# Block-sparse attention with an MLP behind it: the newest value block of each sparse slot issued by SyncE in place of GpSimd

## The chip, the cores and the metric

One core of a Trainium2 chip runs the whole program. The metric is the device time of one execution in microseconds (us); smaller is better. Engines are named as the profile names them: PE (TensorE; PEld is its weight load), DVE (VectorE), ACT (ScalarE), POOL (GpSimd), SP (SyncE). SP computes nothing here: it issues DMAs, one after the other, and waits ahead of each for what the DMA needs.

## What is computed

Attention over 4 batches, 8 heads, 768 tokens and a head width of 64, with a mask in blocks of 32 tokens, and behind it an MLP on the 3072 token rows.

```python
mask = np.abs(blk_i - blk_j) <= 1                     # a window of three blocks
mask = mask | (blk_i == 0) | (blk_j == 0) | (blk_i == n_blocks - 1) | (blk_j == n_blocks - 1)
for qb in range(n_blocks):
    for kb in sampled_blocks[qb]:                     # three sampled blocks for each query block
        mask[qb * 32:(qb + 1) * 32, kb * 32:(kb + 1) * 32] = True
attn = softmax(where(mask, q @ k.T / 8, -1e9))
x = (attn @ v) as rows of 512
out = (s * relu(x @ w_in) ** 2 + b) @ w_out           # 512 -> 2048 -> 512
```

## The kernel before

The work has two stages. The attention stage fills the first 235 us or so, the MLP the rest.

**Slots.** Attention runs in 52 slots, numbered from 0 in the order of the string `T["ORD"]`. Eight are dense (the first and the last query block of a batch, which see every key). The other 44 are sparse: one query block `k` of two batches (a pair `e` of batches) at a time. The sparse query blocks of a pair run in three streams A, B and C (`r` is 0, 1 or 2), taken in turns, and each stream steps by one block. So the window of three neighbours of a stream's next block differs from the last one's by one block: the newest neighbour. The first slot of a stream (`entire`) loads all three neighbours, each later one only the newest. A slot is 4 units (two batches, two parities of heads).

**What a sparse slot does.** PE makes the scores (L979), DVE takes the maximum and adds the mask (L997), ACT the exponential (L1010), PE transposes the probabilities (L1040), DVE and ACT in turn copy them out of PSUM (L1056, L1058), and PE multiplies them with the values (L1106). DVE scales the result (L1112), PE transposes it (L1121), ACT copies it (L1126, tile `xst`), and SP spills it to DRAM (L1133). In one slot of eight blocks there are products with the dense slots' probabilities as well (L1096).

**Values.** Tile `vA` holds one row of three neighbour blocks for each stream and one row of sampled blocks; `vB` holds four more rows of sampled blocks. The window row of a stream is used again by its next slot, three sparse slots later, with one third of it replaced. So the newest neighbour of slot i can be loaded only when the value products of the stream's last slot have read the row. Five rows for sampled blocks go round. `window_v` (L791) issues the load of one neighbour block, 128 KB: for an `entire` slot SP does (21 loads), for the others POOL (38 loads). `sampled_v` (L884) issues the three sampled blocks of a slot: two by SP and the third by POOL, from slot 7 on (L1266).

**What else the two engines issue.** POOL also copies the keys of each slot into `kk` (L913, L924), loads the queries of the sparse slots (L731) and takes part in the decoding of the weights (L88). SP also loads the second pair's keys in 12 pieces during slots 5 to 16 (L714), the queries of the dense slots (L731), the weights (L59, L62), and the attention's results back for the MLP (L401).

**Order.** Each engine works through a fixed list. The lists come from a planner in the kernel, `Plan` (L109): each operation is entered with an engine, a cost in ns, a due time, what it depends on, and what buffers it takes; `Plan.order` then plays the program through with these costs and writes down the order in which things would start. An engine that comes free takes, of what could start first, the one that is due first. The line for the window loads is L1262: on SP and POOL alike the cost is 650, the due time 11 units ahead of the slot (`T["VL"]`). The sampled loads (L1267) are due 13 units ahead and cost 850 on SP. Nothing in the plan runs on the chip: there each engine takes its list in order, and waits at each entry until semaphores say that it may go.

Of the kernel before, what the change touches and what calls it, by code (L numbers as in the profile page):

```python
# [108 lines left out]
class Plan:  # L109
# [15 lines left out]
    def op(self, eng, cost, prio, fn, deps=(), alloc=(), use=(), order=(), nbytes=0, cols=0, late=0.0):  # L125


        o = Plan.Op()
        o.cost, o.prio, o.fn, o.nbytes, o.cols, o.late = cost if isinstance(cost, dict) else {eng: cost}, prio, fn, nbytes, cols, late
        o.pick = isinstance(cost, dict)  # L130
        o.deps, o.order, o.alloc = [d for d in deps if d], [d for d in order if d], alloc
        o.end, o.seq = None, len(self.ops)
        for k in (*alloc, *use):
            self.users.setdefault(k, []).append(o)
        self.ops.append(o)
        return o
# [76 lines left out]
def kernel(  # L213
# [16 lines left out]
    nc = tc.nc  # L230
# [449 lines left out]
    with ExitStack() as es:  # L680
# [12 lines left out]
        for w in T["ORD"].split():  # L693
            if w[1] == "D":
                slots.append(("d", "abcd".index(w[0]), int(w[2]), 0))
            else:
                r = "ABC".index(w[1])
# [37 lines left out]
        def value_tiles():  # L735
            if "A" not in vbox:
                for z in "AB":
                    vbox[z] = gp.tile([P, 4, 2, DM], F32, tag="vg", name=f"v{z}", bufs=2)

        def window_values(r):  # L740
            value_tiles()
            return vbox["A"][:, r]
# [16 lines left out]
        def block_rows(e, j, n=1):  # L759

            return v[2 * e:2 * e + 2, j * BLK:(j + n) * BLK, :].rearrange("a r d -> r a d")

        def newest(k):
            return k - 1 if STREAMS[1] >= k > STREAMS[1] - 8 else k + 1
# [23 lines left out]
        def newcomers(k, entire):  # L788
            return list(range(k - 1, k + 2)) if entire else [newest(k)]

        def window_v(i, entire, m):  # L791

            _, e, k, r = slots[i]
            js = newcomers(k, entire)
            j, p = (js[m], js[m] % 3) if m < len(js) else (0, NSL)
            (nc.sync if entire else nc.gpsimd).dma_start(out=window_values(r)[p::4], in_=block_rows(e, j))


        ident = pers.tile([P, P], F32, name="ident")
# [106 lines left out]
        def window_k(i, entire):  # L906

            _, e, k, r = slots[i]
            kk = keys_tile()
            if entire:  # L910
                nc.gpsimd.tensor_copy(flat(kk[:, r, NSL:NSL + 1]), flat(kts[e][:, :1]))
            for j, p, n in runs(k, entire):
                nc.gpsimd.tensor_copy(flat(kk[:, r, p:p + n]), flat(kts[e][:, j:j + n]))  # L913

        def sampled_k(i, a):

            _, e, k, r = slots[i]
            row = ring_row("k", i)
            kg = keys_tile()[:, NST + row]
            if a == 0 and holds["k"].get(row) != e:  # L920
                holds["k"][row] = e
                nc.gpsimd.tensor_copy(flat(kg[:, NSL:]), flat(kts[e][:, NB - 1:]))
            j = block_register(mybir.EngineType.Pool, k, a)
            nc.gpsimd.tensor_copy(flat(kg[:, a:a + 1]), flat(kts[e][:, bass.ds(j, 1)]))  # L924
# [219 lines left out]
        op = plan.op  # L1144
# [47 lines left out]
        def parts_of(e, blocks):  # L1192
            return [kld[(e, y, p)] for p in sorted({j * KPS[e] // NB for j in blocks}) for y in range(2)]
# [11 lines left out]
        for i, (kind, e, k, r) in enumerate(slots):  # L1205
            u, cost, col = unit_of[i], costs[kind], cols[kind]
# [3 lines left out]
            def queries(which=(0, 1), after=None):  # L1210
                nonlocal pq
                if which[0] in lqs.setdefault(qk, {}):
                    return
                if not dense:
                    firsts.add(qk)
                for a in which:
                    for par in range(2):
                        fresh = not (a or par)
                        pq = op("s" if dense else "g", 450 if dense else 700, max(u - T["QL"], -18.0 if dense else -9.5 if len(firsts) < 3 else -4.5) + 0.01 * par + (9.5 * (u == 0) if dense else 0.02) * a,
                                lambda qk=qk, a=a, par=par: load_q(qk, a, par), alloc=[("qr", qk)] if fresh else [], use=[] if fresh else [("qr", qk)],  # L1220
                                order=[pq] if dense else [pq, after, o_rg if len(firsts) < 3 else first_pk], nbytes=131e3)
                        lqs[qk].setdefault(a, []).append(pq)
# [4 lines left out]
            if dense:  # L1227
                s_use.append((f"kt{e // 2}", e // 2))
            else:
                prev = before.get(r)  # L1230
                if qk[2] == 1:
                    queries((0,), lastk[sorted(lastk)[-2]])
                    queries((1,), pk)
                elif qk[2] == 2:
                    queries((0,), pk)
                entire = k == STREAMS[r]
                first = not before
                blocks = [*range(k - 1, k + 2), 0] if entire else [newest(k)]
                new = [("kk", "kk")] if first else []
                pk = op("g", 1900 if entire else 430, u - T["GK"], lambda i=i, w=entire: window_k(i, w),  # L1240
                        [*parts_of(e, blocks), *(prev[0] if prev else [])], alloc=new, use=[(f"kt{e}", e)] + ([] if first else [("kk", "kk")]), order=[pk])
                s_deps.append(pk)
                first_pk = first_pk or pk
                if qk[2] != 2:
                    queries()
                for a in range(NSL):
                    pk = op("g", 460, u - T["GK"] + 0.1 * (a + 1), lambda i=i, a=a: sampled_k(i, a), [o_rg, *parts_of(e, range(NB))],
                            alloc=[] if a else [("kg", i)], use=[(f"kt{e}", e), ("kk", "kk")] + ([("kg", i)] if a else []), order=[pk])
                    s_deps.append(pk)
                queries((1,), pk)  # L1250
                lastk[i] = pk
                s_use += [("kk", "kk"), ("kg", i)]

                vt = [("vg", "vA"), ("vg", "vB")]
                if first:
                    for m in range(5):
                        pvl = op("s", 450, -8.3 + 0.02 * m, lambda m=m: global_values(m), alloc=[] if m else vt, use=vt if m else [],
                                 order=[pvl], nbytes=(131e3 if m == 4 else 200e3))
                        globs.append(pvl)
                av_deps += globs if e == 0 else []  # L1260
                for m in range(len(newcomers(k, entire)) + (entire and e > 0)):
                    pvl = op("s" if entire else "g", 650, -8.2 + 0.02 * m if first else u - T["VL"] + 0.1 * m, lambda i=i, w=entire, m=m: window_v(i, w, m), prev[1] if prev else [],  # L1262
                             use=vt, order=[pvl], nbytes=131e3)
                    av_deps.append(pvl)
                for a in range(NSL):
                    bg = a == NSL - 1 and i > T["BG"]  # L1266
                    o = op("g" if bg else "s", 700 if bg else 850, u - T["GV"] + 0.1 * a, lambda i=i, a=a, bg=bg: sampled_v(i, a, bg), [o_rg if bg else o_rs],  # L1267
                           alloc=[] if a else [("vs", i)], use=[*vt, *([("vs", i)] if a else [])], order=[pvs], nbytes=131e3)
                    if not bg:
                        pvs = o  # L1270
                    av_deps.append(o)
                pv_at.append((u, pvs))
                if i in T["K1"]:
                    key_piece(1, None, T["K1"].index(i), u - T["GV"] + 0.4, [pvs, spills.get(([None] * 5 + sparse)[sparse.index(i)])])
                av_use = [*vt, ("vs", i)]
# [78 lines left out]
            if k % NBC == 1:  # L1354
                left = sum(sl[0] == "s" and sl[1] == e and sl[2] % NBC == 1 for sl in slots[i + 1:])
                done[e] = done.get(e, 0) + 1
                for b in (2 * e, 2 * e + 1):
                    g = (k - 1) // NBC // (NCK // 2)
# [96 lines left out]
        for k in range(NPL):  # L1455
            g, f = subs[k]
# [6 lines left out]
            if k > 0:  # L1463
                g, f = subs[k - 1]
# [46 lines left out]
    for i in range(NPL, NSUB):  # L1511
        g, f = subs[i]
# [12 lines left out]
    for s in range(S0, B):  # L1525
        a, b = 2 * s, 2 * s + 1
        for p in range(NFC // 2):
            for n in (1, 2, 6, 7, 5, 3, 4):
                to = product(p, s, n)
                i = None  # L1530
# [4 lines left out]
                elif n == 2:  # L1535
                    i = take((a, p), to, part_sums["m1"], ALU.add)
# [4 lines left out]
                elif n == 5:  # L1541
                    i = take((b, p + 8), to, part_sums["u2"], ALU.add)
                    vec.tensor_tensor(out=part_sums["u3"], in0=to, in1=part_sums["u1"], op=ALU.add)  # L1543
                elif n == 3:
                    i = take((b, p), to, part_sums["u3"], ALU.add)
                else:
                    i = take((a, p + 8), part_sums["u2"], to, ALU.subtract)
# [93 lines left out]
```

## Time and profile before

| | us |
|---|---|
| time, median of 3 runs | 752.07 (748.76 to 755.04) |
| time of the profiled execution | 755.85 |
| its span, first to last instruction | 754.2 |
| PE busy | 732.4 (97%) |
| DVE busy | 568.8 (75%) |
| ACT busy | 471.3 (62%) |
| POOL busy | 286.7 (38%) |

Some 1.65 us of the profiled execution's time lie around its span. Waiting and the issue of DMAs aren't counted as busy, so POOL's share says nothing of how long it was held up by either, and SP has no share at all. Matmuls overlap, and PE counts as busy while any of them runs, so PE can be busy and still run below its best pace.

### The profile page before, as it was taken

How to read it: one execution, taken by the hardware profiler on the slowest of the kernel's cores; microseconds unless marked ns; L12 is line 12 of the kernel's file. 1: busy time of each engine (PE TensorE's matmuls, PEld its weight loads, DVE VectorE, ACT ScalarE, POOL GpSimd, SP SyncE). 2: the span in 40 equal slices, each digit the busy share in tenths (PEclk: the TensorE clock that was granted, in tenths of full speed). 3: DMA queues.
4: the chain of work that ended last, by engine and by line, in shares of the span. 5: the costliest groups of instructions: out<-in, count | busy, mean ns of one | idle time of the engine just before them, and what ended most of it. 6: DMA issues, size and time to landing. Idle time of an engine off the chain costs nothing.

```text
span 754.2 us, 21532 instructions
## 1 busy us (share of the span) xinstructions
PE 732.4 (97%) x8032; PEld 624.8 (83%) x8032; DVE 568.8 (75%) x1439; ACT 471.3 (62%) x1140; POOL 286.7 (38%) x477
## 2 busy tenths in 40 slices
PE   7898999999999999999999999999999999999997
PEld 6676766777778898998889888988989988898896
DVE  4866658988787899988886787787677688666752
ACT  3866557989686878788644433675434566345443
POOL 6966657767851221210023222232222322222221
PEclk9999999999999999999999999999999999999999
DMA  9998767867776345536322330233000022000002
GB/s 249 253 272 251 203 184 218 227 190 211 220 207 176 113 135 178 191 112 161 117 59 84 107 96 29 67 114 79 1 1 1 1 63 85 1 1 0 1 1 83
DMA packets 98888, 89.42 MB, mean 119 GB/s; under 512 B 50368, under 2 KB 79936, under 8 KB 98784
## 3 DMA queue, kind: packets, MB, share of 16 engines
q1 hardware_dynamic: 92544, 71.27, 32.5%
q0 software_dynamic: 6096, 16.65, 7.9%
q8 instruction: 63, 1.03, 0.6%
q14 instruction: 41, 0.34, 0.1%
q10 hardware_dynamic: 144, 0.13, 0.0%
HBM read 69.15 MB, written 14.68 MB: 111 GB/s over the span
## 4 chain that ended last, share of the span: by engine, by line
PE 88%; DVE 5%; ACT 3%; issue 2%; DMA 1%; SPq 1%; DVEq 0%; ACTq 0%
PE m L636 21%; PE o L490 11%; PE o L491 11%; PE o L489 11%; PE xs L1106 6%; PE t L1040 6%; PE s L979 6%; PE h L443 3%; PE h L445 3%; PE h L444 3%; PE od L1096 2%; PE t L1121 2%; PE t L1038 1%; DVE ptile L997 1%; PE s L958 1%
## 5 line engine op out<-in xcount | busy, mean ns | idle before, releaser
L467 POOL TENSOR_TENSOR hid<-hid,hid 128x384 fp32r<-128x384 f32 x96 | 105.2, 1096 | 295.8 <-ACT hid L654 286.2
L653 ACT ACTIVATE hid<-hid,sb_b,sb_s 128x384 f32<-128x384 f32 x96 | 68.0, 709 | 153.6 <-DVE hid L647 153.5
L1010 ACT ACTIVATE ptile<-ptile,nm 128x256 f32<-128x256 f32 (+1 forms) x208 | 107.5, 520 | 40.9 <-DVE nm L997 40.9
L997 DVE CUSTOM_DVE_ANT_1 ptile<-s,mt 128x256 f32<-128x256 f32 x176 | 64.4, 420 | 17.3 <-PE s L979 17.0
L491 PE MATMUL o<-woutr,hid 128*128 128x512 f32 x168 | 66.5, 396 | 0.0
L490 PE MATMUL o<-woutr,hid 128*128 128x512 f32 x168 | 66.3, 395 | 0.0
L489 PE MATMUL o<-woutr,hid 128*128 128x512 f32 x168 | 65.3, 389 | 0.0
L636 PE MATMUL m<-wout,win 128*128 128x384 f32 x264 | 61.9, 338 | 0.0
L636 PE MATMUL m<-xp,wop 128*128 128x384 f32 x288 | 58.3, 337 | 0.0
L647 DVE SCALAR_TENSOR_TENSOR hid<-hid 128x384 f32<-128x384 f32 x96 | 54.6, 569 | 3.3
L490 PE MATMUL o<-win,hid 128*128 128x512 f32 x144 | 56.8, 394 | 0.0
L636 PE MATMUL m<-xp,win 128*128 128x384 f32 x288 | 54.6, 337 | 1.4 <-DVE sum L1543 1.4
L1040 PE MATMUL t<-ident,ptile 128*128 128x128 f32 x352 | 54.5, 297 | 0.2
L636 PEld LDWEIGHTS m<-xp,win 128*128 128x128 f32 x288 | 50.9, 188 | 4.1 <-issue 1.7
L654 ACT CAST hid<-hid 128x384 fp32r<-128x384 f32 x96 | 49.4, 514 | 7.8 <-ACT hid L653 0.7
L636 PEld LDWEIGHTS m<-xp,wop 128*128 128x128 f32 x288 | 51.5, 188 | 2.1
L1040 PEld LDWEIGHTS t<-ident,ptile 128*128 128x128 f32 x352 | 45.8, 208 | 6.4 <-issue 0.7
L924 POOL COPY kk<-kt 128x256 f32 x132 | 50.6, 420 | 0.0
L1106 PE MATMUL xs<-vA,pt 128*32 128x64 f32 x1696 | 46.6, 224 | 3.7 <-issue 3.3
L491 PE MATMUL o<-win,hid 128*128 128x512 f32 x126 | 49.8, 395 | 0.0
L489 PE MATMUL o<-win,hid 128*128 128x512 f32 x126 | 49.2, 391 | 0.5 <-ACT ob L505 0.4
L646 DVE TENSOR_TENSOR hid<-m,xrest 128x384 f32<-128x384 f32 x48 | 26.5, 551 | 30.5 <-issue 26.4
(199 smaller groups left out, 1889.4 us busy)
## 6 DMA issues: line engine op xcount, KB each, us to landing
vB<-in_v_dram SPq DMA_DIRECT2D x76, 128.0 KB, 4.1
raw_o<-in_w_out_dram SPq DMA_DIRECT2D x14, 512.0 KB, 3.3
raw_i<-in_w_in_dram SPq DMA_DIRECT2D x12, 512.0 KB, 4.0
vA<-in_v_dram POOLq DMA_DIRECT2D x46, 128.0 KB, 3.6
xd<-xst SPq DMA_DIRECT2D x44, 128.0 KB, 3.7
vA<-in_v_dram SPq DMA_DIRECT2D x42, 128.0 KB, 4.6
sum<-xd SPq DMA_DIRECT2D x12, 384.0 KB, 3.9
out_dram<-ob SPq DMA_DIRECT2D x18, 256.0 KB, 2.3
```

Source lines behind the costliest of these rows:

```text
L467: (eng or nc.vector).tensor_tensor(out=htile(5 + i % 3), in0=t, in1=gh.bitcast(F32), op=ALU.subtract)
L489: nc.tensor.matmul(acc, gh[:, tsl], wout(f, 0), start=first, stop=False)
L490: nc.tensor.matmul(acc, gh[:, tsl], wout(f, 1), start=False, stop=False)
L491: nc.tensor.matmul(acc, gl[:, tsl], wout(f, 0), start=False, stop=last)
L636: nc.tensor.matmul(to, w_, x_, start=(c == 0 and k == 0), stop=(c == 1 and k == 2))
L647: vec.scalar_tensor_tensor(out=t, in0=t, scalar=0.0, in1=t, op0=ALU.max, op1=ALU.mult)
L653: nc.scalar.activation(t, t, AF.Identity, bias=sb_b, scale=sb_s)
L924: nc.gpsimd.tensor_copy(flat(kg[:, a:a + 1]), flat(kts[e][:, bass.ds(j, 1)]))
L997: nc.vector.tensor_tensor_reduce(out=pt, in0=sp, in1=msk, scale=-scale, scalar=FMAX if g == 0 else nm[:, 0:1], op0=ALU.add, op1=ALU.min, a ...
L1010: nc.scalar.activation(pt, pt, AF.Exp, bias=nms[n][:, last:last + 1], scale=-1.0, accum_out=dns[i][:, g, j:j + 1])
L1040: nc.tensor.transpose(tp[:, (2 * j + c) * P:(2 * j + c + 1) * P], src[:, c:SW:2], ident)
L1106: nc.tensor.matmul(xs[quads[pair]], pt[:, c, quads[pair]], vt[:, a, col:col + D], start=(j == 0 and c == 0), stop=(c == 1), tile_position= ...
```

## The change

The newest neighbour's value block of each sparse slot is issued by SP; the planner is told so with the same cost (650) and due time.

```diff
@@ window_v, L796 @@
-            (nc.sync if entire else nc.gpsimd).dma_start(out=window_values(r)[p::4], in_=block_rows(e, j))
+            nc.sync.dma_start(out=window_values(r)[p::4], in_=block_rows(e, j))
@@ the plan, L1262 @@
-                    pvl = op("s" if entire else "g", 650, -8.2 + 0.02 * m if first else u - T["VL"] + 0.1 * m, lambda i=i, w=entire, m=m: window_v(i, w, m), prev[1] if prev else [],
+                    pvl = op("s", 650, -8.2 + 0.02 * m if first else u - T["VL"] + 0.1 * m, lambda i=i, w=entire, m=m: window_v(i, w, m), prev[1] if prev else [],
```

All 38 window loads leave POOL's list and enter SP's. PE's list stays as it is; on DVE and ACT some operations of the weights' decoding and of the attention's end change places.

The first place is SP's list from the spill of slot 6 to that of slot 7. `xst6` is the block of slot 6 that is spilled, L714 a piece of the second pair's keys, and the two groups of L896 are two sampled blocks of slot 12, with the register work ahead of each. Before:

```order
L1133 DMA xd_68<-xst6_965 128x256
L714 DMA kt1_448<-in_k_blk_dram 128x2x256
L896 REGISTER_ALU x2
L896 ISA
L896 DMA vB_212<-in_v_dram 32x2x512
L896 REGISTER_ALU x2
L896 ISA
L896 DMA vB_212<-in_v_dram 32x2x512
L1133 DMA xd_68<-xst7_1061 128x256
```

And now:

```order
L1133 DMA xd_68<-xst6_963 128x256
L796 DMA vA_211<-in_v_dram 32x2x512
L714 DMA kt1_448<-in_k_blk_dram 128x2x256
L896 REGISTER_ALU x2
L896 ISA
L896 DMA vB_212<-in_v_dram 32x2x512
L896 REGISTER_ALU x2
L896 ISA
L896 DMA vB_212<-in_v_dram 32x2x512
L1133 DMA xd_68<-xst7_1060 128x256
```

The window load of slot 10 (L796) stands behind the spill of slot 6, and ahead of the key piece and the sampled blocks. Of the 38, 24 stand right behind the spill of an earlier slot.

The second place is SP's list near the end of attention, from the spill of slot 45 to that of slot 48. `xraw1_0` is a part of the attention's result on its way back for the MLP. Before:

```order
L1133 DMA xd_68<-xst45_4841 128x256
L896 REGISTER_ALU
L896 ISA
L896 DMA vB_212<-in_v_dram 32x2x512
L896 REGISTER_ALU x2
L896 ISA
L896 DMA vB_212<-in_v_dram 32x2x512
L1133 DMA xd_68<-xst46_4946 128x256
L1133 DMA xd_68<-xst47_5040 128x256
L401 DMA xraw1_0_5125<-xd_68 128x12x64
L1133 DMA xd_68<-xst48_5142 128x256
```

And now:

```order
L1133 DMA xd_68<-xst45_4839 128x256
L796 DMA vA_211<-in_v_dram 32x2x512
L896 REGISTER_ALU
L896 ISA
L896 DMA vB_212<-in_v_dram 32x2x512
L896 REGISTER_ALU x2
L896 ISA
L896 DMA vB_212<-in_v_dram 32x2x512
L1133 DMA xd_68<-xst46_4931 128x256
L796 DMA vA_211<-in_v_dram 32x2x512
L1133 DMA xd_68<-xst47_5047 128x256
L796 DMA vA_211<-in_v_dram 32x2x512
```

The first L796 is the window load of slot 48, the next two those of slots 49 and 50; each waits its turn behind a spill.

The third place is DVE's list where the first weights are decoded, between the dense slots in the middle of attention. `xss22` is slot 22's result, `raw_i0` the first piece of weights, `nm89` to `nm91` are the maxima of units 89 to 91, and `pt84` is the probabilities of slot 23. Before:

```order
L1112 TENSOR_TENSOR xss22_2512<-xs_613,rc22_2351 128x256
L85 TENSOR_SCALAR wkhp0_387<-raw_i0_2245 128x512
L87 TENSOR_SCALAR wklp0_534<-raw_i0_2245 128x512
L997 ISA ptile6_80,nm89_2480<-s89_1_2452,mz_114,nm89_2480 128x128x3
L997 ISA nm89_2480 128x1
L1056 COPY pt84_0_2553<-t84_0_2527 128x512
```

And now:

```order
L1112 TENSOR_TENSOR xss22_2513<-xs_613,rc22_2349 128x256
L85 TENSOR_SCALAR wkhp0_387<-raw_i0_2245 128x512
L997 ISA ptile6_80,nm89_2481<-s89_1_2452,mz_114,nm89_2481 128x128x3
L997 ISA nm89_2481 128x1
L1056 COPY pt84_0_2552<-t84_0_2527 128x512
L997 ISA ptile2_79,nm90_2564<-s90_2542,mt_116 128x256
L997 ISA nm90_2564 128x1
L997 ISA ptile2_79,nm91_2571<-s91_2543,mt_116 128x256
L997 ISA nm91_2571 128x1
L87 TENSOR_SCALAR wklp0_534<-raw_i0_2245 128x512
```

The second step of the decoding (L87) has moved behind the copy of slot 23's probabilities (L1056) and two more maxima.

## Rows read from the trace of the kernel before

**Rows 1.** The chain that ended last by engine; then two of the stretches (--windows).

```profile
PE 88%; DVE 5%; ACT 3%; issue 2%; DMA 1%; SPq 1%; DVEq 0%; ACTq 0%
...
core 0: us, PE busy (x) PEld busy (x) DVE busy (x) ACT busy (x) POOL busy (x), PEclk, DMA share, GB/s
...
60.00:80.00 20.00, 16.93 (x477) 12.12 (x467) 12.15 (x54) 12.88 (x46) 13.28 (x30) 1.00 0.87 246
...
160.00:180.00 20.00, 20.00 (x578) 15.22 (x585) 17.89 (x68) 15.86 (x53) 14.01 (x32) 1.00 0.69 207
```

**Rows 2.** Waits of PE, 20 to 240 us, the seven longest: us in total, times, longest.

```profile
PE xs L1106 <- issue: 5.1, 4, 1.8
PE t L1121 <- DVE pt L1056: 1.8, 4, 0.9
PE s L979 <- DVE rc L1019: 1.2, 1, 1.2
PE t L1038 <- DVE nm L997: 1.1, 2, 0.5
PE od L1096 <- issue: 0.9, 2, 0.5
PE od L1121 <- ACT xst L1126: 0.7, 1, 0.7
PE s L979 <- issue: 0.4, 1, 0.4
```

**Rows 3.** Waits of PE's weight loads, 20 to 240 us, for POOL and for loads.

```profile
PEld s L979 <- POOL kk L924: 1.3, 1, 1.3
...
PEld xs L1106 <- DMA vA<-in_v_dram: 0.3, 2, 0.2
```

**Rows 4.** Groups, 20 to 236 us: busy us, mean ns, idle before it.

```profile
L796 POOL DMA_DIRECT2D vA<-in_v_dram x38 | 21.0, 552 | 28.2 <-PE od L1096 20.3 <-PE xs L1106 7.5
```

**Rows 5.** Line L796: ns min/median/max; its DMAs to landing, both queues.

```profile
L796 SPq DMA_DIRECT2D vA<-in_v_dram x21: 598/605/1113, 16.2 to 144.5; - x21
...
DMA to landing us min/median/max: 2.4/4.0/10.7
```

**Rows 6.** DMA issues of value blocks: KB each, median us to landing.

```profile
vB<-in_v_dram SPq DMA_DIRECT2D x76, 128.0 KB, 4.1
...
vA<-in_v_dram POOLq DMA_DIRECT2D x46, 128.0 KB, 3.6
...
vA<-in_v_dram SPq DMA_DIRECT2D x42, 128.0 KB, 4.6
```

**Rows 7.** Timeline of SP from slot 6's spill to slot 7's: start, us.

```profile
51.39 1.16 SPq L1133 DMA_DIRECT2D xd<-xst  x1
52.60 0.43 SPq L714 DMA_DIRECT2D kt<-in_k_blk_dram  x1
53.43 1.55 SPq L896 DMA_DIRECT2D vB<-in_v_dram  x2
55.09 0.53 SPq L1133 DMA_DIRECT2D xd<-xst  x1
```

**Rows 8.** Timelines of POOL (slot 10's window load) and PE (slot 10's first value product).

```profile
49.59 0.55 POOL L796 DMA_DIRECT2D vA<-in_v_dram  x1 [0.41 <-PE xs L1106]
...
59.53 0.32 PE L1106 MATMUL xs<-vA,pt 128*32 128x64 f32 x8
```

**Rows 9.** Timelines of SP (slot 45's spill) and PE (slot 48's value products).

```profile
215.64 1.32 SPq L1133 DMA_DIRECT2D xd<-xst  x1
...
221.69 1.29 PE L1106 MATMUL xs<-vA,pt 128*32 128x64 f32 x64
```

**Rows 10.** Timelines of DVE and PE where the first weights are decoded.

```profile
119.05 1.39 DVE L87 TENSOR_SCALAR wklp<-raw_i 128x512 uint16<-128x512 uint16 x1
...
121.60 0.44 PE L1121 MATMUL t<-ident,xss 128*128 128x128 f32 x2 [0.94 <-DVE pt L1056]
```

**Rows 11.** Waits of SP, 30 to 235 us: us in total, times, longest.

```profile
SPq L1133 <- ACT xst L1126: 34.8, 22, 3.7
```

## The prediction

> **What bounds the kernel now.** I read the chain of waits first, because it says which engine the end hangs on: PE holds 88% of it, and no other engine more than 5% [rows 1]. So a saving counts only where PE waits. The change touches the attention stage alone, and there the busy time by stretch is the next view: between 60 and 80 us PE is busy 16.93 of 20 us, between 160 and 180 us all 20 [rows 1]. The second half of attention is thus bound by PE itself, and only the first half leaves something to win, while the DMA engines stand at a share of 0.87.
>
> The third view is what PE waited for from 20 to 240 us [rows 2]. Its seven longest items sum to 11.2 us: 5.1 + 0.9 + 0.4 = 6.4 us under "issue", where the profile shows nothing that PE waited for, and 1.8 + 1.2 + 1.1 + 0.7 = 4.8 us for DVE and ACT. POOL is not among them, nor a value load. The weight loads ahead of the matmuls show a little more: 1.3 us once for POOL's key copy, and 0.3 us in two pieces for blocks in vA [rows 3].
>
> POOL's side looks worse than it is. Its 38 window loads take 21.0 us, and 28.2 us of waiting stand ahead of them, mostly for PE to finish reading the row [rows 4]. That is nearly 50 us of POOL's time, but it is time that an engine off the chain spends waiting for the engine on it.
>
> **What is removed from POOL.** 38 loads at 552 ns are 21.0 us, and the 28.2 us of waits go too [rows 4]. What stands behind them on POOL are key copies, sampled blocks, queries and the weights' low words, which all come earlier by that. Who waits for these? PE for 1.3 us in total, in one piece [rows 3]. It is a wait for keys, and keys depend on PE's scores too, so the gain lies between 0 and 1.3 us. I take 0, because a single wait in 44 sparse slots shows that POOL's copies are normally in time.
>
> **What is added to SP.** 38 loads at a median of 605 ns, the price of the 21 that SP already issues [rows 5], are 23 us of SP's time. On average SP has room: between 30 and 235 us it waits 34.8 us for copies of results alone, ahead of its spills [rows 11]. But from slot 5 to slot 16 it has the second pair's keys to issue as well, and there it has none: from slot 6's spill to slot 7's, 3.70 us, it issues for 1.16 + 0.43 + 1.55 = 3.14 us, and the 0.56 us between are the register work and dispatch of the sampled blocks [rows 7]. In such a slot each window load pushes all that follows back by 0.6 us: the key piece, two sampled blocks and the next spill. None of these is needed soon (the sampled blocks behind slot 6's spill belong to slot 12), so I cost their delay at nothing. The cover is the distance of their slot; if it went, each would cost PE what it comes late.
>
> What can be late is the window load itself, which now also waits for SP's turn. Two places:
>
> Slot 10. POOL issued it at 49.59, and PE reads it at 59.53 [rows 8]. Now it follows slot 6's spill, which starts at 51.39 and takes 1.16 us [rows 7]. The loads of slots 8 and 9 stand ahead on the same queue, 2 x 0.6 = 1.2 us more if SP had no gap to take them. So it is issued at about 51.39 + 1.16 + 1.2 = 53.8 and must land within 59.5 - 53.8 = 5.7 us. Blocks in vA that SP issued took 4.6 us at the median, those of vB 4.1 [rows 6]: in time by about 1 us.
>
> Slot 48. It follows slot 45's spill, which ends at 215.64 + 1.32 = 216.96; PE begins with the values at 221.69 [rows 9]. There are 4.7 us against 4.6 or 4.1. In the best case nothing is lost; with the longest landing that the line shows, 10.7 us [rows 5], it is 6 us late. That one fell into the loads of the start, so I go by the medians and take a loss of 0.3 us here.
>
> One rule of the Trainium skill weighs on this place. The rows say that a vA block lands 3.6 us after its issue on POOL and 4.6 us after one on SP [rows 6]. The page "DMA: Bandwidth & Descriptors" (Specifications, and "Issuing engine by pattern") holds the path of SyncE to be the faster one in general, about 0.6 us to the first byte where GpSimd's takes about 1 us. By the page, slot 48's block would land 3.6 - 0.4 = 3.2 us after its issue (an estimate from that page and the row), and nothing would be lost; by the rows it is a tie. The trace doesn't agree with the page here, and I go by the trace, since SP's loads stand behind others in its queue.
>
> **What moves on DVE and ACT.** Where the first weights are decoded, one step (L87) takes 1.39 us on DVE ahead of the copy that PE needs, and PE waits 0.94 us for that copy [rows 10]. The order now has that step behind the copy, so I take back 0.9 us. The other moves are of the same kind, decoding steps placed a slot later and an exponential behind some copies at the end of attention. Each could cost or save what this one does; I take 0 for them, with bounds of -0.9 and +0.9.
>
> **The sum**, against the profiled execution's 755.85 us (span 754.2, and 1.65 around it): 0 from POOL's relief, 0 from SP's occupancy, +0.3 at slot 48, -0.9 at the decoding. That is -0.6, so 755.2 us. The median before is 752.07, 3.8 us below the profiled execution. The same step on the median gives 751.5 us. The three runs before spread from 748.76 to 755.04, so nothing of this size can be told from no change: about 1%, 7.5 us, is what a measurement of this kernel resolves.
>
> Ends of the range for the forecast alone: below, -1.3 (POOL), -0.9 and -0.9 (decoding) and -0.3 (the two vA waits): 752.07 - 3.4 = 748.7. Above, slot 48 late by 2 (half way from none to four), +0.9, and 1 us at slot 10: 752.07 + 3.9 = 756.
>
> **Rivals.**
>
> 1. POOL's relief is worth more than its waits show. For it: DVE and ACT wait in turn for PE, and a key copy that comes earlier could pull all three forward; PE's 4.8 us for DVE and ACT would go, 747.3 us. If the 6.4 us under "issue" went as well, because window loads off POOL's queue leave the DMA engines another pattern, it would be 752.07 - 11.2 = 740.9 us. Against it: the waits under "issue" name neither POOL nor a load, the bytes moved are the same, and POOL's waits come from PE's reads, which don't move.
>
> 2. The window loads come late: slower. The mechanism is one queue. On POOL a window load had only sampled blocks and queries beside it; on SP it stands behind spills, key pieces and sampled blocks, both in SP's list and on the way. It decides from the point where issue to landing takes more than the 5.7 us of slot 10 or the 4.7 us of slot 48. At 10.7 us, the longest seen [rows 5], the loads of the key stretch are 5 us late; a stall there moves every later need back by the same, so it is paid once, and 6 us more at slot 48: 752.07 + 11 - 0.9 = 762 us. For it: 4.6 against 3.6 us [rows 6], the full SP [rows 7] and a DMA share of 0.87 [rows 1]. Against it: medians, not the longest, decide, and PE has slack at nearly all other slots. The Trainium skill speaks for this rival: by "DMA: Bandwidth & Descriptors", section "Queues, rings and completion order", a DMA engine takes turns between queues, so a load with a queue of its own doesn't stand behind another's backlog; the 3.6 against 4.6 us agree with it.
>
> 3. The waits under "issue" shift by chance. They are 6.4 us [rows 2]; doubled, the time is 758.5, without them 745.7. Both lie near the 1% bounds and widen the range.
>
> **How the numbers follow.** My forecast, no change that can be told: 0.70 (748.7 to 756). Rival 1: 0.10, of which its full form, the only one past 1%, 0.06. Rival 2: 0.10 (762), nearly all of it past 1%. Rival 3: 0.10, half on either side, and some of each half past 1%. Faster by over 1% (below 744.5): 0.06 + 0.03 + 0.02 for a mix of both = 0.11. Slower by over 1% (above 759.6): 0.09 + 0.03 = 0.12. Within: 0.77. The range for 8 in 10 takes in rival 3's lower end and most of the way to rival 2: 745.5 to 759.
>
> **What would show it.** In the profile after, the waits of POOL should have lost the 28 us ahead of L796, and those of SP should have gained waits for PE at L796. PE's waits should name a value load at slot 48 with under 1 us, or not at all, and no wait of 0.94 us for DVE at the first decoding. Waits of PE for vA of several us in the key stretch, or landings of vA near 6 us and more, would make me wrong on the slow side. PE's waits for DVE and ACT falling to near nothing would do so on the fast side.

## The result, and the profile after

| | median, us | runs | lowest to highest |
|---|---|---|---|
| before | 752.07 | 5 | 748.47 to 755.04 |
| after | 759.68 | 5 | 757.57 to 763.62 |

The ratio is 1.0105, with a 95% interval from 1.0069 to 1.0141: the change makes the kernel about 1% slower, some 7.9 us. The forecast was 751.5 us with a range from 745.5 to 759. The profiled execution of after took 759.68 us, its span is 757.6 us; that of before (755.85) lay above all five runs of the table, so the two spans differ by only 3.4 us. I therefore read places and causes from the traces, and sizes from the medians.

The chain of after by engine, then the two stretches of [rows 1] (stretch, then busy time of PE, PEld, DVE, ACT and POOL, the granted clock, DMA share and GB/s):

```profile
PE 88%; DVE 6%; ACT 2%; DMA 2%; issue 1%; SPq 1%; DVEq 0%; ACTq 0%
...
60.00:80.00 20.00, 14.18 (x416) 11.06 (x417) 9.91 (x45) 11.02 (x39) 11.99 (x28) 0.92 0.90 254
160.00:180.00 20.00, 19.96 (x582) 15.09 (x578) 17.39 (x68) 15.53 (x52) 10.26 (x27) 1.00 0.64 193
```

PE still holds the chain. The stretch from 60 to 80 us has lost 2.75 us of PE's work against [rows 1] (14.18 for 16.93); the stretch from 160 to 180 us has lost nothing. What PE waited for in after, 20 to 240 us (total, times, longest), beside [rows 2]:

```profile
PE xs L1106 <- DMA vA<-in_v_dram: 5.8, 2, 4.5
PE xs L1106 <- issue: 1.7, 3, 1.0
PE t L1040 <- issue: 1.2, 1, 1.2
PE s L979 <- DVE rc L1019: 1.2, 1, 1.2
PE t L1121 <- DVE pt L1056: 1.2, 2, 0.8
```

The first line is new: twice the value product waits for a block in vA. The waits under "issue" are fewer than in [rows 2]; more of that below. The weight loads tell the same, beside [rows 3]:

```profile
PEld xs L1106 <- DMA vA<-in_v_dram: 7.0, 6, 4.7
...
PEld s L979 <- POOL kk L924: 1.5, 2, 1.3
```

POOL is rid of L796, but its waits are not gone, beside [rows 4]. The waits of POOL, 20 to 236 us:

```profile
POOL kk L913 <- PE s L979: 58.2, 31, 3.2
```

In before this line read 24.6 us in 20 waits. So the 28.2 us ahead of the window loads became 33.6 us more ahead of the next key copies, which wait for PE as well: POOL got ahead and stood still one instruction later. PE's wait for POOL's keys is what it was, 1.5 against 1.3 us. (POOL's busy time fell from 286.7 to 264.4 us with 38 instructions fewer, so the profile does count POOL's DMA issues as busy, contrary to what stands with the table of before.)

Line L796 in after, beside [rows 5], and SP's wait for results, beside [rows 11]:

```profile
L796 SPq DMA_DIRECT2D vA<-in_v_dram x59: 598/621/1616, 16.2 to 231.9; - x59
...
  PEld xs L1106: 7.0, 6
  PE xs L1106: 5.8, 2
...
DMA to landing us min/median/max: 2.6/4.1/5.8
```

```profile
SPq L1133 <- ACT xst L1126: 10.4, 9, 2.8
```

The transfer itself is no slower (4.1 us from issue to landing at the median, 5.8 at most), but SP's waits for results, which the prediction took for its room, fell from 34.8 to 10.4 us. Some slots of SP in the key stretch, from a spill to the next, beside [rows 7], and the window load of slot 13 (start, us):

```profile
55.59 0.38 SPq L1133 DMA_DIRECT2D xd<-xst  x1
56.07 1.18 SPq L796 DMA_DIRECT2D vA<-in_v_dram  x1
...
64.72 1.19 SPq L1133 DMA_DIRECT2D xd<-xst  x1
66.01 0.61 SPq L796 DMA_DIRECT2D vA<-in_v_dram  x1
66.68 0.58 SPq L714 DMA_DIRECT2D kt<-in_k_blk_dram  x1
67.66 1.55 SPq L896 DMA_DIRECT2D vA<-in_v_dram  x2
69.32 1.61 SPq L1133 DMA_DIRECT2D xd<-xst  x1
...
72.43 0.62 SPq L796 DMA_DIRECT2D vA<-in_v_dram  x1
...
74.11 0.50 SPq L1133 DMA_DIRECT2D xd<-xst  x1
```

From the spill of slot 6 at 55.59 to that of slot 10 at 74.11 there are four slots: 4.63 us each, where [rows 7] had 3.70. PE's pace is seen where it transposes the results of the same two slots:

```profile
48.80 0.44 PE L1121 MATMUL t<-ident,xss 128*128 128x128 f32 x2
...
64.21 0.44 PE L1121 MATMUL t<-ident,xss 128*128 128x128 f32 x2
```

That is 15.41 / 4 = 3.85 us. In before the same four slots took SP 14.29 / 4 = 3.57 us and PE 17.00 / 4 = 4.25 us (two score groups there ran 0.5 and 0.7 us longer than usual). So SP went from faster than PE to slower than PE: the lag of a spill behind its transposes, which in before shrank from 3.9 us at slot 6 to 1.2 at slot 10, grew in after from 6.8 to 9.9 us. Slot 10's load is issued at 56.07, 6.5 us later than in [rows 8], and is just in time (PE reads at 59.91 and names no DMA). Slot 13's, at 72.43, isn't. PE of after:

```profile
69.59 0.32 PE L1106 MATMUL xs<-vA,pt 128*32 128x64 f32 x8 [1.37 <-DMA vA<-in_v_dram]
...
77.71 0.44 PE L1106 MATMUL xs<-vA,pt 128*32 128x64 f32 x8 [4.45 <-DMA vA<-in_v_dram]
...
79.57 1.98 PE L1040 MATMUL t<-ident,ptile 128*128 128x128 f32 x8
81.49 1.96 PE L979 MATMUL s<-kk,qr_5s 64*32 64x256 f32 x32
```

Here stands the loss: 1.37 us at slot 12 and 4.45 us at slot 13. Slot 13's place had long been free (slot 10's products ran from 59.91 to about 61), so the load waited for its turn on SP. It landed by 77.71, at most 5.3 us behind its issue; with the median of 4.1 us PE would still have waited over 3 us. And it isn't all, as the stretches show:

```profile
76.00:78.00 2.00, 0.29 (x12) 0.29 (x16) 0.00 (x0) 0.00 (x0) 0.00 (x0) 0.68 1.02 278
78.00:80.00 2.00, 2.00 (x66) 1.83 (x58) 0.29 (x1) 0.00 (x0) 0.03 (x1) 0.50 1.02 273
80.00:82.00 2.00, 2.00 (x24) 1.47 (x30) 1.08 (x4) 0.41 (x1) 0.52 (x1) 0.50 0.52 149
```

After PE's pause the granted clock is 0.50, the level of 1.2 GHz, up to about 83 us: eight transposes take 1.98 us where 1.22 is usual. From slot 13's products to slot 14's, at 83.81, it is 6.10 us, where an undisturbed slot without dense products takes 3.58 (52.38 to 55.96), so the slow clock cost some 2.5 us more. PE's busy time of 2.00 in 2 us hides this; the clock column shows it.

The two other places of the prediction:

```profile
219.75 0.65 SPq L1133 DMA_DIRECT2D xd<-xst  x1
220.49 0.63 SPq L796 DMA_DIRECT2D vA<-in_v_dram  x1
...
224.24 0.80 PE L1106 MATMUL xs<-vA,pt 128*32 128x64 f32 x41
...
121.03 0.44 PE L1121 MATMUL t<-ident,xss 128*128 128x128 f32 x2
```

Slot 48 [rows 9] is in time, 3.75 us from issue to use, and the decoding's wait of 0.94 us [rows 10] is gone.

### The profile page after: what moved, and what is told of

Same layout as the page of the kernel before. It is cut to its first block, busy times and chain, and to the rows that moved or that the text cites. A ratio compares the mean times of both kernels' runs of the same rounds, so it can differ in the third digit from the quotient of the medians.

```text
span 757.6 us, 21534 instructions
## 1 busy us (share of the span) xinstructions
PE 733.1 (97%) x8032; PEld 625.2 (83%) x8032; DVE 566.2 (75%) x1439; ACT 470.5 (62%) x1140; POOL 264.4 (35%) x439
## 4 chain that ended last, share of the span: by engine, by line
PE 88%; DVE 6%; ACT 2%; DMA 2%; issue 1%; SPq 1%; DVEq 0%; ACTq 0%
PE m L636 21%; PE o L490 11%; PE o L491 11%; PE o L489 11%; PE t L1040 6%; PE xs L1106 6%; PE s L979 6%; PE h L443 3%; PE h L445 3%; PE h L444 3%; PE od L1096 2%; PE s L958 2%; PE t L1121 2%; PE t L1038 2%; DMA vA<-in_v_dram 1%
```

## The experiments

The theories that the expectations name: A, SP is full in the key stretch and its lag makes the window loads late; B, the loads of the later slots cost; C, the planner's new order of the other engines costs, not who issues (D is its form in which VectorE and ScalarE are the cause); F, PE stalls on its own instruction stream at fixed places. Ratios are to the kernel before, which ran again beside each batch (its medians lay from 751.72 to 752.43 us); they aren't quotients of two medians, so that 758.51 us has 1.0066 and 757.61 us 1.0085. I compare ratios. Medians are in us.

| run | median | ratio (95% interval) |
|---|---|---|
| engine alone, all / late half | 761.72 / 756.16 | 1.0113 (1.0074 to 1.0153) / 1.0052 (1.0027 to 1.0078) |
| order alone, twice | 755.08, 755.24 | 1.0038 (1.0018 to 1.0058), 1.0036 (1.0012 to 1.0061) |
| order alone, early / late half | 754.58 / 756.39 | 1.0024 (1.0003 to 1.0045) / 1.0050 (1.0030 to 1.0070) |
| SP from slot 17 / up to 16 | 755.47 / 757.05 | 1.0045 (1.0022 to 1.0068) / 1.0063 (1.0041 to 1.0084) |
| keys on GpSimd / keys spread | 755.14 / 759.44 | 1.0046 (1.0024 to 1.0068) / 1.0103 (1.0080 to 1.0126) |
| exchange | 753.69 | 1.0014 (0.9995 to 1.0033) |
| before shifted by 32 / 64 / 96 | 755.00 / 758.51 / 754.20 | 1.0028 (1.0005 to 1.0052) / 1.0066 (1.0042 to 1.0089) / 1.0028 (0.9998 to 1.0058) |
| shifted by 64: order / exchange / after | 757.61 / 758.23 / 764.15 | 1.0085 (1.0062 to 1.0108) / 1.0068 (1.0044 to 1.0092) / 1.0163 (1.0126 to 1.0200) |

**The engine and the order apart.** The planner orders by its own clock, so the issuing line and the planner's entry can be changed one without the other.

```diff
 engine alone: before, with window_v on nc.sync; the planner still enters the load for "g"
 order alone: after, with window_v on nc.gpsimd again; the planner still enters it for "s"
```

> The order of TensorE, VectorE and ScalarE is that of the kernel before, instruction for instruction; only the 38 window loads stand in SyncE's row, at the places in time where the planner had put them for GpSimd. Theory A (in the key stretch, slots 7 to 15, SyncE is full, every window load adds to its lag, and the loads come late): still slower than before, 756 to 760 us, with TensorE waiting 3 us or more for DMA vA at L1106 between 60 and 80 us. Theory C (the new order of the other engines costs the time): 751 to 753.5 us, as before. Theory B (the loads of the later sparse stretches, slots 33 to 51, cost it): 756 to 760 us, but the waits for vA stand behind 180 us.

> The order of TensorE, VectorE and ScalarE is that of the changed kernel, instruction for instruction; only the window loads are issued by GpSimd again. Theory A: no wait for vA on TensorE over 0.5 us between 60 and 80 us, and 750.5 to 754 us. Theory C (the order): 757 to 760 us. Theory B: 750.5 to 754 us, like A.

> The run that changed the order alone, once more, for its size and for a second profile: 753.5 to 756.5 us if its 3.0 us were real, 751 to 753 us if they were chance. In the profile: a real cost of the order must show as waits of TensorE for VectorE or ScalarE that the kernel before has not, 2 us or more in all between 121 and 242 us.

The engine alone costs 1.13%, and its profile has theory A's wait (3.82 us at 76.17); its time is 1.7 us above the range that A had. But the order alone, with no wait for vA at all, costs 0.38% and 0.36%: the order has a part, about 2.8 us, though less than the 757 to 760 us that C had named. The profile sign that I had asked of it (2 us of new waits for VectorE or ScalarE) is not there.

**The halves.** The cut is at slot 16.

```diff
-nc.sync.dma_start(out=window_values(r)...
+(nc.sync if entire or i > 16 else nc.gpsimd).dma_start(out=window_values(r)...
```

The planner's entry follows the same condition. The second run has i <= 16. The engine alone for the late half has this line in the kernel before, without the entry; the order alone by halves has the entry without the line.

> GpSimd issues the window loads up to slot 16 (the stretch with the second pair's keys), SyncE those from slot 17 on; the planner plans with it. Theory A: 750.5 to 754 us, the waits for vA between 60 and 80 us gone. Theory B: the loss stays, 757 to 760 us, and TensorE falls behind the kernel before from 180 us on by 3 us or more. Theory C: the order behind 121 us is nearly that of the changed kernel, 756 to 760 us.

> The other half: SyncE issues the window loads up to slot 16, GpSimd those from slot 17 on. Theory A: the loss stays, 756 to 760 us, with the wait of 3 us or more for vA at L1106 near 78 us. Theory B: 751 to 753.5 us by the fast half, though the wait near 78 us is there, since TensorE had made it up again by 121 us in the changed kernel's profile. Theory C: 751 to 754 us.

> As in the run that changed the engine alone, the order of TensorE, VectorE and ScalarE is that of the kernel before, but SyncE issues only the window loads from slot 17 on, at GpSimd's places in time; those up to slot 16 stay on GpSimd. The two halves have so far cost 3.4 us (late) and 5.0 us (early) by the medians. If the late half's loss comes from the new order of the other engines (theory C for the late half): 751 to 753 us, no loss. If it comes from SyncE's issuing of the late loads (theory B): 754.5 to 757 us, with waits for vA behind 180 us.

> GpSimd issues all window loads, as before; the planner orders everything as if SyncE issued those from slot 17 on. It parts the 3.0 us by which the order alone was slower. If the new order of VectorE, ScalarE and TensorE behind 121 us costs it (theory C for the late half): 754 to 757 us. If the order costs nothing there (theory B or chance): 751 to 753 us.

> The other half of it: GpSimd issues all window loads, and the planner orders everything as if SyncE issued those up to slot 16. Theory A (the early loss is SyncE's lag, and no matter of order): 751 to 753 us. If the order costs in the early half: 754 to 757 us.

The early half alone brings the stall back, in a time within A's range (SP from slot 17 is 1.5 us above its range, by about what the order's late half costs). PE with SP up to slot 16:

```profile
80.31 0.44 PE L1106 MATMUL xs<-vA,pt 128*32 128x64 f32 x8 [4.92 <-DMA vA<-in_v_dram]
```

What the issuing engine costs is the difference between two runs with the same order: early 0.63 - 0.24 = 0.39%, late 0.45 - 0.50 = -0.05%, each give or take about 0.3% by the intervals. So SP's issuing costs in the key stretch, and no cost can be seen behind it, as long as the planner knows of it. The parts don't add up exactly: the two halves of the order sum to 0.74%, while the whole order measured 0.37%. Sizes from such differences are rough. Where the planner doesn't (the engine alone, late half), it costs 0.52%, and by a way that I hadn't thought of. ACT, PE and SP of that run:

```profile
133.73 0.27 ACT L1126 COPY xst<-od 128x128 f32<-128x128 f32 x1 [3.27 <-DMA xd<-xst]
```

```profile
134.63 0.97 PE L958 MATMUL s<-kt,qr_0d 64*64 64x384 f32 x4 [3.04 <-ACT wkhp L1050]
```

```profile
124.62 3.32 SPq L796 DMA_DIRECT2D vA<-in_v_dram  x5
...
128.66 0.93 SPq L1137 DMA_DIRECT2D xd<-xst  x2
```

SP's lag made spills late (this one follows its copy by 5.8 us, in before by 3.2), ACT found no free buffer for the next result, and PE waited for ACT. The wait for vA behind 180 us that the expectation named for theory B is there too, once, with 1.52 us at 225.46. The lag comes out at whichever reader has the least slack: the next window load in the key stretch, a result's buffer here.

**SP's queue made shorter.** If the count of transfers per slot is the cause, any other twelve or forty that leave SP should do.

```diff
 keys on GpSimd: after, with the second pair's key pieces (load_k and its entry) on GpSimd
 keys spread:
-    "K1": (5, 6, 7, 8, 9, 10, 11, 12, 13, 14, 15, 16)
+    "K1": (5, 6, 8, 9, 11, 12, 14, 15, 17, 18, 20, 21)
 exchange:
-    bg = a == NSL - 1 and i > T["BG"]
+    bg = a >= NSL - 2 and i > T["BG"]
```

> The changed kernel, but the 12 key pieces of the second pair are issued by GpSimd, so that SyncE has in slots 5 to 16 as many transfers to issue as before. Theory A (SyncE is full there, and its lag makes the window loads late): no wait for vA over 1 us between 60 and 80 us, and 5 us less than the changed kernel: 753 to 757 us. Rival (a window load on SyncE's queue lands late whatever else is queued there): the wait of 3 us or more near 78 us stays, 758 to 762 us.

> The changed kernel, but the 12 key pieces of the second pair go with two of every three slots from 5 to 21 instead of with each of slots 5 to 16; SyncE issues as many transfers in all, but fewer in each stretch. Theory A: the lag gathers a third of a key piece less per slot, the wait near 78 us falls to under 1 us, 753 to 757 us. Rival (the landing on SyncE's queue, not its lag): the wait stays, 758 to 762 us.

> An exchange: SyncE issues all window loads, as in the changed kernel, and from slot 7 on GpSimd issues two of a slot's three sampled blocks instead of one, so that both queues have as many transfers as in the kernel before. Theory A in both halves (SyncE's count of transfers per slot is what costs): no wait of TensorE for vA over 0.5 us and 751 to 753.5 us. If it matters that a window load, which waits for TensorE's last use of its place, stands in SyncE's row at all: 755 us or more. If GpSimd's waiting at window loads (28.2 us in the kernel before) was worth something: below 750 us.

With the keys on GpSimd the waits of PE for vA are gone, and 60 to 80 us are full again:

```profile
60.00:80.00 20.00, 19.57 (x561) 14.31 (x554) 14.16 (x59) 14.04 (x51) 16.45 (x36) 1.00 0.83 245
```

The time falls by 0.59% to 1.0046, and what stays is near the order's part (0.37%). The rival, a landing that is slow on SP's queue whatever else is in it, falls. The spread keys don't help, against what I expected of theory A. SP shows why: the two spills below lie six slots apart, 26.64 / 6 = 4.44 us each, while PE took 22.56 / 6 = 3.76 us in the same slots (transposes at 51.53 and 74.09), so the lag still grows; two of PE's waits follow.

```profile
53.72 1.26 SPq L1133 DMA_DIRECT2D xd<-xst  x1
...
80.36 0.52 SPq L1133 DMA_DIRECT2D xd<-xst  x1
```

```profile
76.72 0.32 PE L1106 MATMUL xs<-vA,pt 128*32 128x64 f32 x8 [2.20 <-DMA vA<-in_v_dram]
...
118.06 0.32 PE L1106 MATMUL xs<-vA,pt 128*32 128x64 f32 x8 [2.12 <-DMA vA<-in_v_dram]
```

The exchange is the sharpest of the three: all 38 window loads stay on SP, and 1.0014 can't be told from before; in its profile only PE's weight loads still name vA, with 1.0 us in six waits, none over 0.2. Nor is it the landing:

```profile
DMA to landing us min/median/max: 2.4/4.5/9.9
```

Its window loads land later than those of after (median 4.1), and yet PE doesn't wait. A window load may stand on SP here; one transfer per slot too many may not. Its 753.69 us lies 0.2 us above the range of theory A. It doesn't beat the kernel before either, and no run did.

**What is chance, and what is place.** The first run is the kernel before once more; the others put small matmuls into the warm-up at the start, whose results nothing uses.

```diff
-op("p", 430, T["FP"], lambda: warm_up(2), ...        # 8 matmuls of 128 columns
+op("p", 430, T["FP"], lambda: warm_up(10, 24), ...   # 40 of 24 columns: 64 passes more
```

> The kernel before, profiled once more, to see what of its profile is chance. If TensorE's waits on nothing visible (6.4 us between 20 and 240 us in its first profile) are chance: their sum and places differ by 2 us or more and the span goes with them, 747 to 753 us, while its waits for VectorE and ScalarE (4.8 us there) come back within 1 us. If they belong to the program: both come back within 1 us.

> The kernel before, with 64 more matmul passes in TensorE's warm-up at the start (40 small ones instead of 8 large ones, results unused), so that everything behind stands 64 passes later in TensorE's stream. In all profiles so far, TensorE's waits on nothing visible inside a group of equal matmuls stand at passes 334, 460, 713, 967, 1221, 1347, 1474 and so on, always multiples of about 127 apart. Theory F (they are waits for the instruction stream itself, at fixed places of it): they stay at these counts, and so move by half a step against the groups they stand in. Rival (they belong to what the groups read): they stay with the groups, at counts 64 higher. Time under F: 749 to 757 us, as the places fall; under the rival 751 to 753.5 us.

> The run that changed the order alone, with the same 64 passes in front. Theory F: its extra waits behind 121 us (1.7 and 2.4 us in two profiles, against 0.5 and 0.8 us in the kernel before) change with the places, and its distance to the shifted kernel before is no longer 2 to 4 us: under 1.5 us, or over 4.5 us. Theory D (the order costs by what VectorE and ScalarE do later): the distance to the shifted kernel before stays at 2 to 4 us.

> The kernel before with 32 more passes in TensorE's warm-up instead of 64. Theory F (the stalls on the instruction stream stand at fixed counts about 127 passes apart, and what they cost depends on the groups that they fall in): the stalls stand again at counts such as 1347, 1474, 1601; the time is neither that of the kernel before (751.9) nor that of the shift by 64 (758.5) by rule, anything from 749 to 759 us. Rival (the 40 small warm-up passes themselves cost the 5 us, by a later start or a cold engine): 24 of them cost less than 40, 752 to 756 us, and the loss stands before 20 us.

> The same with 96 more passes. Theory F: no order by size: the time may lie below that of the shift by 64, 749 to 758 us. Rival (the warm-up passes themselves): above that of the shift by 64, 759 us or more.

> The exchange (all window loads on SyncE, two of three sampled blocks on GpSimd) with the 64 passes in front, whose own waits of this kind came to 2.7 us behind 121 us. Theory A with F: no wait for vA, and a time within 3 us of 753.7 us on either side, moved by the places of the stalls alone; below 750 us it would beat both kernels.

> The changed kernel with the 64 passes in front. Theory A (SyncE's full queue) is not a matter of places: the waits for vA between 60 and 80 us are there again, 3 us or more, and it is 3 to 7 us slower than the order alone with the same shift (757.6): 760.5 to 764.5 us. If the whole loss of the change was a matter of where the stalls fall: within 2 us of the shifted kernel before, 756.5 to 760.5 us.

The kernel before, again, took 753.38 us; PE's waits of 20 to 240 us:

```profile
PE xs L1106 <- issue: 5.2, 4, 2.4
PE t L1121 <- DVE pt L1056: 1.8, 4, 0.9
...
PE s L979 <- DVE rc L1022: 1.2, 1, 1.2
PE t L1038 <- DVE nm L997: 1.1, 2, 0.5
PE od L1121 <- ACT xst L1126: 0.7, 1, 0.7
PE s L979 <- issue: 0.4, 1, 0.4
```

The four waits for VectorE and ScalarE come back to the tenth of [rows 2] (one under another line). The "issue" ones sum to 5.6 us against 6.4, but at other places: the largest is 2.39 us at 37.87, where the first profile has none. With 64 passes in front, a stall splits a group of equal matmuls that runs in one piece (32 passes in 1.09 us) in both profiles of before. A pass is one record of PE in the trace. The shifted kernel:

```profile
146.75 0.83 PE L979 MATMUL s<-kk,qr_3s 64*32 64x256 f32 x17
...
149.27 0.66 PE L979 MATMUL s<-kk,qr_3s 64*32 64x256 f32 x15 [1.69 <-issue]
```

Counted off the trace's records of passes, the stalls of before, both profiles together, stand at 334, 460, 586, 713, 967, 1221, 1347, 1474, 1982 and 3746, 4381; those of the shifted kernel at 840, 1094, 1348, 1475, 1602, 1729, 3115, 4127, 4635, 4762, 5016. It is one grid with a step of 126 or 127, and it stays with the count, not with the groups: theory F holds for the places. At which points of the grid PE stalls, and for how long, changes from profile to profile. The page of after lists, among its DMA queues:

```profile
q8 instruction: 63, 1.03, 0.6%
```

63 packets for 8032 passes are 127.5 passes each, about the step of the grid. So these are most likely waits of PE for the next packet of its own instructions; that is argued from the count, as no row names the releaser.

The shifts cost 0.28, 0.66 and 0.28% (the last can't be told from nothing), not in the order of their size, and PE's first score starts at 10.94, 11.32 and 10.66 us against 10.80 and 11.11 without: it is the place, not the added work. So moving all of PE's instructions by half a step of the grid was worth up to 5 us here. The 758.51 us is half a us above the range that I had given F.

Place doesn't explain the order's 2.8 us, though: the order alone leaves PE's list as it is, so its groups stand at the same counts as in before. Its extra "issue" waits are on the grid: behind 121 us its two profiles have 1.7 and 2.4 us of them, those of before 0.5 and 0.8, and they include one at 2743, where neither profile of before has any. And little else sets its profiles apart: take PE's "issue" waits of 20 to 240 us off the times of the profiled executions, and before is at 749.5 and 747.8 us, the order alone at 747.3 and 747.6, its halves at 748.4 and 748.6. The same for after, with its waits for vA off as well, gives 750.4 us, and 2.5 us of that are the slow clock. Whether the new order on DVE and ACT brings these stalls about or chance did in so few profiles, no run shows. Shifted alike, order and before differ by 0.85 - 0.66 = 0.19%, give or take 0.3%, which fits 0.37% as well as nothing; by the medians the order is even 0.9 us faster. The order's part stays open.

SP's queue is no matter of place. Shifted, after shows PE's waits for vA again, larger:

```profile
PE xs L1106 <- DMA vA<-in_v_dram: 8.5, 5, 4.1
```

and is 1.63 - 0.66 = 0.97% behind before, and 0.78% behind the order alone; unshifted these were 1.05 and 0.68%. The longest, 4.1 us, is again the one of slot 13, at 77.33; 1.8 us are at slot 48. The exchange equals before with the shift too (1.0068 and 1.0066), though its 758.23 us is 1.5 us above the range that I had given.

## Why the prediction was wrong

The loss of 1.05% has two parts. SP's issuing costs 1.05 - 0.37 = 0.68%, about 5 us, give or take 0.4% (0.78% when shifted, 1.13% in the order of before), and the planner's new order of the other engines 0.37%, about 2.8 us. The first part's cause is shown: the waits for vA go when another transfer leaves SP. The second's is open. The 1% that I took for the least that can be told was too coarse: the interval is 0.36% to a side.

- **POOL's relief at 0:** right. Its 28.2 us of waits turned into 33.6 us at the key copies, PE's wait for POOL stayed at 1.5 us, and rival 1 fell.
- **SP's occupancy: "I cost their delay at nothing".** This is the step that failed: the term that stands in the sum as 0 measured about 5 us. I added the loads ahead of slot 10's once, and to a spill of slot 6 that I left where before had it, at 51.39; so I had slot 10's load "issued at about 53.8". The spill went out at 55.59 and the load at 56.07. It was still in time, but the lag grew by 0.8 us with each slot, and at slot 13 PE waited 4.45 us. I had the row that warned of it: 3.70 us per slot [rows 7] and one more load of 0.6 us make 4.3 us at least, no less than the 4.25 us that PE took for the same slots in before, so that SP could not make up a lag. With its long issues (1.19, 1.61 us) SP took 4.63, and PE, undisturbed, 3.85. I never set SP's time per slot against PE's.
- **What a stall costs:** I counted only its length. The clock at half pace for about 5 us behind it came on top, some 2.5 us.
- **Slot 48 at +0.3:** about right for after, which has no wait there; but its margin was as thin as the 4.7 us had said: four other profiles wait 0.9 to 1.8 us at that place, the planner knowing of the load in two of them (the spread keys, after shifted) and not in the other two (engine alone, all and late half).
- **The decoding at -0.9, the other moves at 0:** the first is right as seen at its place, but not to be found in the time: the order as a whole was slower by 2.8 us, beyond my bound of +0.9. PE has no new waits for DVE or ACT from it, so this term failed too, and why is open.
- **Landing on SP, 4.6 us by the median:** it is 4.1 over all 80 such loads, so it was mainly the turn in SP's list that was late, not the way. (The Trainium skill, "DMA: Bandwidth & Descriptors", "Issuing engine by pattern", holds SyncE's path to be the faster one; after doesn't show it either, with 4.1 us for SP's vA loads and 3.5 us for the vB loads that POOL issues.) For rival 2 I had named both, "in SP's list and on the way": in the main the list it was.
- **Rival 2,** with a chance of 0.10, is nearest to what happened, with 762 us forecast and 759.68 measured. Its place (the key stretch) and its mechanism (one queue, in SP's list) were right. Its condition was not: it asked for landings of more than 5.7 us, and priced 10.7; the longest of all window loads took 5.8 us, and slot 13's late block at most 5.3. Its price is near by luck: the 6 us at slot 48 that it counted didn't come, and the order's part, which it did not count, did. "PE has slack at nearly all other slots" shouldn't have counted against it, since a lag that grows eats any slack.
- **Rival 3:** the "issue" waits do move by chance from run to run. They went the other way in the profile of after (3.5 us for 6.4), so they aren't the loss that it shows.
- **The signs:** PE's waits for vA of several us in the key stretch, which were to make me wrong on the slow side, came; the landings of vA kept to 4.1 us at the median. SP's list of waits has gained PE at L796, as expected, with 15.0 us in 27 waits (30 to 235 us).

## What to carry to other kernels

When work moves to another queue, compare that queue's time per step with the pace of the engine that it feeds. Here, with the queue at or above that pace, the lag grew step by step until the transfer with the least slack stalled the bound engine, and the stall cost clock as well. If a transfer has to move, try to exchange it for one with more slack, so that each queue's count per step stays; here that cost nothing that could be measured. And before a difference under 0.7% between two orders of this kernel is put down to a cause, look at PE's "issue" waits in their profiles: a plain shift of PE's stream alone moved the time by that much.

## What the runs showed of the hardware

- PE has waits that name no releaser at counts of passes on a grid with a step of 126 or 127, 0.2 to 3 us each, 1 to 9 us in all per profile, at changing points of the grid; the instruction queue's 63 packets for 8032 passes have about the same step. 64 passes in front of the kernel before made it 0.66% slower. That PE waits there for its own instructions is argued from the counts.
- After a pause of PE of 4.45 us in a stretch that had run at full clock, the granted clock was 0.50 for about 5 us.
- A DMA's issue on SP takes 0.4 to 0.6 us at most places, but in the key stretch of after four of twenty (55.6 to 74.1 us) took 1.2 to 1.6 us. The profile lists these as waits, partly for what had long been done (slot 9's spill, issued at 69.32 for 1.61 us, with 1.5 us for ACT, whose copy of that result had ended at 61.04). Why, no run here shows.
